# Where one copy stands in ScalarE's queue: the second expert layer of a decay-attention kernel

## The chip, the cores and the metric

The kernel runs on one core of a Trainium2 chip. A core has five engines with a queue of instructions each: TensorE (PE; its weight loads are listed as PEld), VectorE (DVE), ScalarE (ACT), GpSimd (POOL) and SyncE (SP), which issues the DMAs. Each works through its queue in order, and semaphores hold an instruction back until what it needs is there. The metric is the device time of one execution in microseconds (us), the median of several.

## The reference

Three steps follow each other, in float32: a linear attention with a decaying state, and two expert layers with different activations.

```python
for t in range(S):                                   # S = 768; 4 batches, 8 heads of 48
    cur = np.einsum('bhd,bhe->bhde', u[None] * kt, vt)
    y[:, :, t] = np.einsum('bhd,bhde->bhe', rt, state + cur)
    state = w[None, :, :, None] * state + np.einsum('bhd,bhe->bhde', kt, vt)
# x: 3072 tokens x 384
h = x @ w_in;  r = np.maximum(h, 0.0);  x = (r * r) @ w_out          # layer 1, d_ff 2048
h = x @ w_in2; g = h - np.tanh(h);      out = g @ w_out2             # layer 2, d_ff 2048
```

The change lies in layer 2 alone.

## The kernel before

The 3072 tokens are cut into NB = 6 blocks of TB = 512, and the 2048 hidden features into NF = 16 groups of 128. A **unit** is one block and one group: 96 units in layer 1, then 96 in layer 2. All matrix products are made of float32 numbers split into a rounded high part and the rest, the low part; a product then takes three terms: high by high, and the two mixed ones.

For a unit of layer 2, `gemm1` (L496) makes the hidden values h in a bank of PSUM, with nine matmuls of 128x512 (three slices of the 384 inputs, three terms). Three banks (3, 4, 5) take turns. `act2` turns h into g = h - tanh(h) and splits it; `gemm2_2` (L645) multiplies g by the second weights, nine matmuls again, and accumulates into three banks for the whole block. `evac2` (L656) copies these out at the end of a block, and SyncE writes them to memory.

Because h - tanh(h) loses its digits where h is small, `act2` computes two things and picks one. ScalarE makes y = h squared (L590), th = tanh(h) (L591), two shifted squares q1 (L593) and q2 (L596) and the sign of y - 0.25 as a mask (L599). VectorE makes hy = PK h y (L592), multiplies it by q1 + PC (L600) and by q2 + PD (L606), which is a polynomial in h for small values; it makes h - th (L595), and puts that over hy where the mask says so (L611). Then ScalarE rounds hy into the high part (L617, `act2_high`) and VectorE subtracts that to get the low part (L623, `act2_low`).

The work on one unit is spread over three calls of `act2`. In the call for unit n, L606 and L611 (`act2_poly`, `act2_pick`) and L617 work on unit n-1, and L623 on unit n-2. So ScalarE's queue in one call reads: y, th, q1, q2, mask of n, high part of n-1. VectorE's reads: L592 of n, L606 of n-1, L595 of n, L611 of n-1, L623 of n-2, L600 of n. `act2_flush` finishes the last unit.

The order on every queue is the order of the program text (`tc.manual_schedule()`). The waits are put in by the framework: an instruction waits for those before it in the text, on other engines, whose data it uses or whose buffer it takes over. `look` sets how far the first products run ahead in layer 2:

```python
while nf < len(units) and nf <= n + look(n):
    front(nf)          # gemm1 and act2 of unit nf; look is 3 in layer 2
    nf += 1
```

and after it, in the same round, comes `gemm2_2` of unit n. So TensorE's queue in a quiet stretch reads: first product of n+3, second of n, first of n+4, second of n+1.

Around that, `prep_x2` loads the next block's input in three slices and splits it, with a VectorE copy (L568) and a GpSimd subtraction (L569) in three of the 16 rounds (f = 5, 7, 9). In the first block's rounds f = 1 and 2 the last two weight tiles of layer 2 are still made (L101 on ScalarE, L107 on GpSimd). Buffers: hy has 3, y, th, q1, q2 and mask have 2 each, the high and low parts 4 each.

Of the kernel before, what the change touches and what calls it, by code (L numbers as in the profile page):

```python
# [13 lines left out]
ALU = mybir.AluOpType  # L14
# [5 lines left out]
PK = 0.0069430512315236536  # L20
# [5 lines left out]
def decay_attention_moe_moe_kernel(  # L26
# [10 lines left out]
    nc = tc.nc  # L37
# [464 lines left out]
    def split(g):  # L502
        hi = gp.tile([128, TB], F32R, tag="ghi", name="ghi", bufs=4)
        lo = gp.tile([128, TB], F32R, tag="glo", name="glo", bufs=4)
        return hi, lo
# [75 lines left out]
    def act2(j, f):  # L581
        pool = p2["pool"]
        h = hq.pop((2, j, f))
        n = j * NF + f
        mk = lambda n: pool.tile([128, TB], F32, tag=n, name=n)
        y, th, q1, q2 = (mk(n) for n in ("y", "th", "q1", "q2"))
        hy = pool.tile([128, TB], F32, tag="hy", name="hy", bufs=3)
        mask = pool.tile([128, TB], U8, tag="mask", name="mask")
        st2[n] = (q2, hy, mask, th)
        nc.scalar.activation(out=y, in_=h, func=AF.Square)  # L590
        nc.scalar.activation(out=th, in_=h, func=AF.Tanh)  # L591
        nc.vector.scalar_tensor_tensor(out=hy, in0=h, scalar=PK, in1=y, op0=ALU.mult, op1=ALU.mult)  # L592
        nc.scalar.activation(out=q1, in_=y, func=AF.Square, bias=p2["ba"], scale=1.0)  # L593
        act2_poly(n - 1)
        nc.vector.tensor_tensor(th, h, th, op=ALU.subtract)  # L595
        nc.scalar.activation(out=q2, in_=y, func=AF.Square, bias=p2["bb"], scale=1.0)  # L596
        act2_pick(n - 1)
        act2_low(n - 2)
        nc.scalar.activation(out=mask, in_=y, func=AF.Sign, bias=p2["bm"], scale=1.0)  # L599
        nc.vector.scalar_tensor_tensor(out=hy, in0=q1, scalar=PC, in1=hy, op0=ALU.add, op1=ALU.mult)  # L600
        act2_high(n - 1)

    def act2_poly(n):
        if n >= 0:
            q2, hy, mask, th = st2[n]
            nc.vector.scalar_tensor_tensor(out=hy, in0=q2, scalar=PD, in1=hy, op0=ALU.add, op1=ALU.mult)  # L606

    def act2_pick(n):
        if n >= 0:
            q2, hy, mask, th = st2[n]  # L610
            nc.vector.copy_predicated(hy, mask, th)  # L611

    def act2_high(n):
        if n >= 0:
            hy = st2[n][1]
            hi, lo = split(hy)
            nc.scalar.activation(out=hi, in_=hy, func=AF.Copy)  # L617
            st2[n] = (hy, hi, lo)

    def act2_low(n):  # L620
        if n >= 0:
            hy, hi, lo = st2.pop(n)
            nc.vector.tensor_tensor(lo, hy, hi.bitcast(F32), op=ALU.subtract)  # L623
            gq[(2, *divmod(n, NF))] = (hi, lo)

    def act2_flush():
        n = NB * NF - 1
        act2_poly(n)
        act2_low(n - 1)
        act2_pick(n)  # L630
        act2_high(n)
        act2_low(n)
# [57 lines left out]
    def front(n):  # L690
        layer, j, f = units[n]
        gemm1(layer, j, f)
        (act1 if layer == 1 else act2)(j, f)
        if n == len(units) - 1:
            act2_flush()
# [256 lines left out]
```

## Time and profile before

| | us |
|---|---|
| median of 3 runs | 962.3 (962.3 to 963.05) |
| the profiled execution, its own time | 963.27 |
| its span, first to last instruction | 961.5 |
| TensorE busy (matmul) | 922.7 |
| VectorE busy | 722.9 |
| ScalarE busy | 637.6 |
| GpSimd busy | 250.8 |
| mean granted TensorE clock | 0.988 |

The first row is what a change is measured by. The span leaves out 1.8 us around the first and last instruction of that execution. Busy times are sums over the whole span, in which the attention, layer 1 and layer 2 follow each other; layer 2 begins at about 527 us with its first product. An engine that is busy for most of the span need not be the one that sets the pace in each stage.

### The profile page before, as it was taken

Reading aid. Unit: us, or ns where it says so; the run is one execution under the profiler, and the core shown is the slowest. Engines: PE = TensorE matmul, PEld = TensorE weight load, DVE = VectorE, ACT = ScalarE, POOL = GpSimd, SP = SyncE. Lnnn points to the kernel's source line nnn. Section 1 sums busy time; section 2 is a strip of 40 time slices with the busy share of each in tenths; the row PEclk is TensorE's granted clock in tenths of the full one; section 3 lists DMA queues with packets and bytes.
Section 4 is the critical chain, followed back from the end, with each engine's and each line's share of the span. In section 5 each row is a group of like instructions: output and inputs, shape, how many; then the busy total and the mean of one; then the engine's idle time right before and its main releaser. Section 6 shows DMA issues by size and latency. Waiting matters only on the chain.

```text
span 961.5 us, 13137 instructions
## 1 busy us (share of the span) xinstructions
PE 922.7 (96%) x4748; PEld 741.5 (77%) x4748; DVE 722.9 (75%) x1201; ACT 637.6 (66%) x1150; POOL 250.8 (26%) x216
## 2 busy tenths in 40 slices
PE   7889999999999999999999999999999999999997
PEld 6767778888888888888888777777777777777775
DVE  6898957854882884550377789899899898898886
ACT  3656565555554554553688887877877887878885
POOL 5833325654563654443110011001000010010000
PEclk7999999999999999999999999999999999999999
DMA  8754512212121221201563100100100100100000
GB/s 248 232 168 159 191 59 65 87 52 77 54 93 38 85 60 49 79 7 40 199 230 132 55 12 1 56 11 1 56 12 1 55 12 1 56 11 1 34 1 33
DMA packets 28800, 67.50 MB, mean 70 GB/s; under 512 B 4928, under 2 KB 11968, under 8 KB 28736
## 3 DMA queue, kind: packets, MB, share of 16 engines
q1 hardware_dynamic: 28592, 66.47, 21.5%
q8 instruction: 37, 0.61, 0.3%
q10 hardware_dynamic: 144, 0.20, 0.1%
q14 instruction: 27, 0.22, 0.1%
HBM read 55.25 MB, written 9.44 MB: 67 GB/s over the span
## 4 chain that ended last, share of the span: by engine, by line
PE 45%; DVE 33%; ACT 17%; issue 2%; POOL 1%; DMA 1%; DVEq 0%; ACTq 0%; POOLq 0%
PE h L496 19%; PE acc L536 19%; DVE hy L592 7%; DVE hy L606 7%; DVE hy L611 7%; ACT ghi L617 6%; DVE th L595 6%; ACT th L591 5%; ACT y L590 5%; PE sc L290 2%; PE y L429 2%; PE y L422 2%; DVE w L107 1%; DVE am L342 1%; DVE raw L92 1%
## 5 line engine op out<-in xcount | busy, mean ns | idle before, releaser
L496 PE MATMUL h<-xt,w 128*128 128x512 f32 x864 | 215.9, 395 | 0.0
L496 PE MATMUL h<-xs,w 128*128 128x512 f32 x864 | 212.9, 391 | 0.0
L496 PEld LDWEIGHTS h<-xs,w 128*128 128x128 f32 x864 | 162.2, 188 | 36.2
L496 PEld LDWEIGHTS h<-xt,w 128*128 128x128 f32 x864 | 161.3, 190 | 33.8 <-DVE xt L406 0.4
L536 PE MATMUL acc<-ghi,w 128*128 128x512 f32 x576 | 153.3, 398 | 0.4 <-ACT x2s L552 0.4
L510 ACT ACTIVATE g<-h 128x512 f32<-128x512 f32 x96 | 57.2, 596 | 143.8 <-PE h L496 143.7
L645 PE MATMUL o<-ghi,w 128*128 128x512 f32 x576 | 150.6, 392 | 2.0 <-ACT ob L656 2.0
L645 PEld LDWEIGHTS o<-ghi,w 128*128 128x128 f32 x576 | 108.4, 189 | 26.5 <-ACT ob L656 4.1
L536 PEld LDWEIGHTS acc<-ghi,w 128*128 128x128 f32 x576 | 104.9, 188 | 23.9 <-ACT g L510 1.1
L516 POOL TENSOR_TENSOR glo<-g,ghi 128x512 fp32r<-128x512 f32 x64 | 85.7, 1339 | 136.2 <-ACT ghi L513 61.8
L617 ACT ACTIVATE ghi<-hy 128x512 fp32r<-128x512 f32 x96 | 60.7, 632 | 83.9 <-DVE hy L611 83.9
L569 POOL TENSOR_TENSOR xs<-x2f,xs 128x512 fp32r<-128x512 f32 x18 | 24.5, 1360 | 337.1 <-PE o L645 204.8
L592 DVE SCALAR_TENSOR_TENSOR hy<-h,y 128x512 f32<-128x512 f32 x96 | 66.4, 692 | 53.6 <-ACT th L591 53.5
L645 PE MATMUL o<-glo,w 128*128 128x512 f32 x288 | 93.1, 425 | 13.6 <-DVE glo L623 13.6
L536 PE MATMUL acc<-glo,w 128*128 128x512 f32 x288 | 84.5, 395 | 7.7 <-DVE glo L525 7.7
L645 PEld LDWEIGHTS o<-glo,w 128*128 128x128 f32 x288 | 47.9, 189 | 44.9 <-DVE glo L623 39.7
L324 POOL TENSOR_TENSOR am<-ident,bt 128x512 f32<-128x512 f32 x44 | 50.5, 1148 | 89.8 <-DVE bt L308 70.1
L606 DVE SCALAR_TENSOR_TENSOR hy<-q,hy 128x512 f32<-128x512 f32 x96 | 73.2, 763 | 0.1
L273 DVE TENSOR_TENSOR fr<-rkt,fr 112x256 fp32r<-112x256 f32 x30 | 38.8, 1294 | 42.9 <-ACT fr L272 42.9
L536 PEld LDWEIGHTS acc<-glo,w 128*128 128x128 f32 x288 | 54.0, 189 | 21.6 <-DVE glo L525 10.7
L611 DVE COPY_PREDICATED hy<-mask,th 128x512 f32<-128x512 uint8 x96 | 69.9, 728 | 0.0
L593 ACT ACTIVATE q<-y,ba 128x512 f32<-128x512 f32 x96 | 69.6, 725 | 0.0
(105 smaller groups left out, 1388.8 us busy)
## 6 DMA issues: line engine op xcount, KB each, us to landing
raw<-in_w_dram SPq DMA_DIRECT2D x32, 768.0 KB, 4.3
rkt<-in_rk_dram SPq DMA_DIRECT2D x23, 448.0 KB, 4.9
kvt<-in_nat_dram SPq DMA_DIRECT2D x23, 384.0 KB, 5.0
x2d<-x2s SPq DMA_DIRECT2D x18, 256.0 KB, 2.3
x2f<-x2d SPq DMA_DIRECT2D x18, 256.0 KB, 3.1
out_dram<-ob SPq DMA_DIRECT2D x18, 256.0 KB, 2.2
rnt<-in_nat_dram SPq DMA_DIRECT2D x23, 192.0 KB, 2.4
xt<-ys SPq DMA_DIRECT2D x120, 16.0 KB, 1.8
```

The source lines that it names most:

```text
L324: nc.gpsimd.tensor_tensor(am_t[d].rearrange("p (a z) t -> p a z t", a=2), ident[:, None, None, :].to_broadcast([128, 2, 2, C]), hd.to_broa ...
L496: nc.tensor.matmul(h, lhsT=w_in(layer, f, part, kk), rhs=x[:, xpart, kk, :], start=(n == 0), stop=(n == 3 * KK - 1),)
L510: nc.scalar.activation(out=g, in_=h, func=AF.Relu)
L516: nc.gpsimd.tensor_tensor(lo, g, hi.bitcast(F32), op=ALU.subtract)
L536: nc.tensor.matmul(acc[j][m], lhsT=w_out(1, f, part, m * 128, (m + 1) * 128), rhs=g, start=(f == 0 and n == 0), stop=(f == NF - 1 and n == 2),
L592: nc.vector.scalar_tensor_tensor(out=hy, in0=h, scalar=PK, in1=y, op0=ALU.mult, op1=ALU.mult)
L593: nc.scalar.activation(out=q1, in_=y, func=AF.Square, bias=p2["ba"], scale=1.0)
L595: nc.vector.tensor_tensor(th, h, th, op=ALU.subtract)
L606: nc.vector.scalar_tensor_tensor(out=hy, in0=q2, scalar=PD, in1=hy, op0=ALU.add, op1=ALU.mult)
L611: nc.vector.copy_predicated(hy, mask, th)
L617: nc.scalar.activation(out=hi, in_=hy, func=AF.Copy)
L645: nc.tensor.matmul(acc[j][m], lhsT=w_out(2, f, part, m * 128, (m + 1) * 128), rhs=g, start=(f == 0 and n == 0), stop=(f == NF - 1 and n == 2),
```

## The change

In `act2`, the call of `act2_high` moves from the end to the place behind the first Square, and works on unit n-2 in place of n-1. The VectorE instruction L592 is issued before the tanh in the text, where it was issued after it. `act2_flush` gets the call of `act2_high` that the last unit now lacks. ScalarE's queue in one call then reads: y of n, high part of n-2, th, q1, q2, mask of n. VectorE's queue keeps its order. The arithmetic is the same.

```diff
@@ -588,8 +588,9 @@
         mask = pool.tile([128, TB], U8, tag="mask", name="mask")
         st2[n] = (q2, hy, mask, th)
         nc.scalar.activation(out=y, in_=h, func=AF.Square)
+        act2_high(n - 2)
+        nc.vector.scalar_tensor_tensor(out=hy, in0=h, scalar=PK, in1=y, op0=ALU.mult, op1=ALU.mult)
         nc.scalar.activation(out=th, in_=h, func=AF.Tanh)
-        nc.vector.scalar_tensor_tensor(out=hy, in0=h, scalar=PK, in1=y, op0=ALU.mult, op1=ALU.mult)
         nc.scalar.activation(out=q1, in_=y, func=AF.Square, bias=p2["ba"], scale=1.0)
         act2_poly(n - 1)
         nc.vector.tensor_tensor(th, h, th, op=ALU.subtract)
@@ -598,7 +599,6 @@
         act2_low(n - 2)
         nc.scalar.activation(out=mask, in_=y, func=AF.Sign, bias=p2["bm"], scale=1.0)
         nc.vector.scalar_tensor_tensor(out=hy, in0=q1, scalar=PC, in1=hy, op0=ALU.add, op1=ALU.mult)
-        act2_high(n - 1)
 
     def act2_poly(n):
         if n >= 0:
@@ -625,6 +625,7 @@
 
     def act2_flush():
         n = NB * NF - 1
+        act2_high(n - 1)
         act2_poly(n)
         act2_low(n - 1)
         act2_pick(n)
```

## The prediction

> **What bounds the kernel now.** I read the page first, then busy time by stage, then the chain of waits in order of time, then the timeline of single units of layer 2.
>
> ```profile
> span 961.5 us, 13137 instructions
> ...
> PE 922.7 (96%) x4748; PEld 741.5 (77%) x4748; DVE 722.9 (75%) x1201; ACT 637.6 (66%) x1150; POOL 250.8 (26%) x216
> ...
> PE h L496 19%; PE acc L536 19%; DVE hy L592 7%; DVE hy L606 7%; DVE hy L611 7%; ACT ghi L617 6%; DVE th L595 6%; ACT th L591 5%; ACT y L590 5%; PE sc L290 2%; PE y L429 2%; PE y L422 2%; DVE w L107 1%; DVE am L342 1%; DVE raw L92 1%
> ...
> L592 DVE SCALAR_TENSOR_TENSOR hy<-h,y 128x512 f32<-128x512 f32 x96 | 66.4, 692 | 53.6 <-ACT th L591 53.5
> ```
>
> A TensorE (PE) that is busy 96% looks like the bound, but the chain holds no layer-2 matmul worth naming (L645 is absent): it runs through L590, L591, L592, L606, L595, L611 and L617, on ScalarE (ACT) and VectorE (DVE). By stages (columns: window, its length, then busy time of PE, PEld, DVE, ACT, POOL, granted clock, DMA share, GB/s):
>
> ```profile
> 461.00:531.00 70.00, 70.00 (x310) 57.96 (x309) 45.73 (x63) 56.28 (x85) 6.27 (x4) 1.00 0.47 167
> ...
> 684.20:754.50 70.30, 68.23 (x290) 52.82 (x288) 61.88 (x101) 56.44 (x100) 3.90 (x3) 1.00 0.07 23
> ...
> 895.00:957.50 62.50, 60.28 (x251) 46.96 (x250) 51.72 (x85) 47.48 (x84) 0.00 (x0) 0.97 0.04 13
> ```
>
> The end of layer 1 has no PE gap at a full clock; a block of layer 2 fits fewer matmuls (288 against some 310) into the same time. The chain in order of time gives both paces:
>
> ```profile
> 502.67 2.04 PE h L496 x9
> ...
> 684.24 1.56 ACT ob L656 x3
> 754.51 1.55 ACT ob L656 x3
> ```
>
> Nine matmuls in 2.04 us, 0.227 each, so a unit (18 matmuls) needs 4.08 us and a block of 16 units 65.3. A layer-2 block takes 754.51 - 684.24 = 70.27. Inside one unit (start, duration, engine, line, what; in brackets the idle time before it):
>
> ```profile
> 702.55 0.58 ACT L590 ACTIVATE y<-h 128x512 f32<-128x512 f32 x1
> ...
> 703.02 0.59 ACT L591 ACTIVATE th<-h 128x512 f32<-128x512 f32 x1
> ...
> 703.50 0.72 ACT L593 ACTIVATE q<-y,ba 128x512 f32<-128x512 f32 x1
> 703.64 0.69 DVE L592 SCALAR_TENSOR_TENSOR hy<-h,y 128x512 f32<-128x512 f32 x1 [0.50 <-ACT th L591]
> 704.12 0.72 ACT L596 ACTIVATE q<-y,bb 128x512 f32<-128x512 f32 x1
> 704.25 0.68 DVE L606 SCALAR_TENSOR_TENSOR hy<-q,hy 128x512 f32<-128x512 f32 x1
> 704.73 0.71 ACT L599 ACTIVATE mask<-y,bm 128x512 uint8<-128x512 f32 x1
> 704.85 0.68 DVE L595 TENSOR_TENSOR th<-h,th 128x512 f32<-128x512 f32 x1
> ...
> 705.45 0.73 DVE L611 COPY_PREDICATED hy<-mask,th 128x512 f32<-128x512 uint8 x1
> 706.08 0.68 DVE L623 TENSOR_TENSOR glo<-hy,ghi 128x512 fp32r<-128x512 f32 x1
> 706.22 0.63 ACT L617 ACTIVATE ghi<-hy 128x512 fp32r<-128x512 f32 x1 [0.77 <-DVE hy L611]
> 706.67 0.68 DVE L600 SCALAR_TENSOR_TENSOR hy<-q,hy 128x512 f32<-128x512 f32 x1
> 706.76 0.58 ACT L590 ACTIVATE y<-h 128x512 f32<-128x512 f32 x1
> 706.81 0.53 PEld L645 LDWEIGHTS o<-glo,w 128*128 128x128 f32 x3 [0.26 <-DVE glo L623]
> ```
>
> The period is 706.76 - 702.55 = 4.21, and it is a ring: L590, L591, then L592 (0.03 after tanh ends, not after the square ends at 703.13), L606, L595, L611, then L617 (0.04 after L611 ends), then the next L590. ScalarE stands idle 0.77 in it, VectorE 0.50, and PE waits at the low part because the ring is 0.13 slower than PE's 4.08.
>
> **The change part by part.** No instruction is added or removed. Three things move.
>
> *L617 one unit later.* It now follows L590 of unit n and works on unit n-2, whose L611 was issued a unit earlier, so the 0.77 wait is gone, and L590 no longer stands behind L611. Its consumers: L623 of n-2, four places later on VectorE in the same unit, and TensorE's product of n-2, which comes after two more groups of nine matmuls (4.08). The high part is ready 0.47 + 0.63 = 1.10 after L590 starts, so this hides; from 2.98 us of lateness of ScalarE on, each further one would be a stop of TensorE. The copy moved past no DMA: ScalarE and VectorE issue none here.
>
> *L592 ahead of tanh.* Its order on VectorE is as before; what changes is which of two readers of bank h goes first. I take it that L592 follows L590 at the measured 0.03, and that tanh, which reads the same bank, then waits for L592 to end at the measured 0.04. Queued behind tanh are q1, q2 and mask, and L595 waits for tanh on VectorE. From L592's start t:
>
> - ScalarE: tanh t + 0.69 + 0.04 = 0.73; then start to start 0.48, 0.62 and 0.61 to q1, q2, mask, and 0.61 to the next L590: 2.32 together. L590 to L592 is 0.61. Its ring: 0.73 + 2.32 + 0.61 = 3.66.
> - VectorE: L595 at 0.73 + 0.59 + 0.03 = 1.35 (without a wait 1.21), then 0.60 to L611, 0.63 to L623, 0.59 to L600, 0.60 to the next L592: 3.77.
>
> The trace of before doesn't show that reversed wait. Bounds: no wait at all makes VectorE 3.63; L592 waiting for L617 too is the first rival. I take 3.77, since the two readers stand one behind the other in all 96 units. The Trainium skill, "PSUM — Partial Sum Buffer", section "PSUM bank collisions raise a hardware error", says that ScalarE and VectorE may not touch one bank in the same partitions at once, reads against reads included. It speaks against the change, for the wait is then only turned round; by it the ring is 3.77, without it 3.63. The 0.03 agrees.
>
> Both are under 4.08, so **TensorE sets the pace**, with 0.31 per unit to recover from disturbances. The low part of n comes from unit n+2's stretch of VectorE work. After the first product of n+2, TensorE has nine matmuls (second product of n-1), nine (first of n+3) and six with the high part of n before it needs the low part: 24 x 0.227 = 5.44. It is ready 0.03 + 0.61 + (1.35 + 0.60 + 0.63) + 0.68 = 3.90 after it. So a unit may be 1.5 us late before TensorE stops.
>
> *Disturbances.* Evacuation of a block, the casts for the next block, and the last weight conversions:
>
> ```profile
> 613.97 1.55 ACT L656 ACTIVATE ob<-o 128x512 f32<-128x512 f32 x3
> ...
> 615.40 0.61 ACT L590 ACTIVATE y<-h 128x512 f32<-128x512 f32 x1
> ```
>
> ```profile
> 711.48 0.42 DVE L568 CAST xs<-x2f 128x512 fp32r<-128x512 f32 x1
> ...
> 712.06 0.69 DVE L592 SCALAR_TENSOR_TENSOR hy<-h,y 128x512 f32<-128x512 f32 x1 [0.16 <-ACT th L591]
> ...
> 712.67 1.22 DVE L606 SCALAR_TENSOR_TENSOR hy<-q,hy 128x512 f32<-128x512 f32 x1
> ```
>
> Evacuation costs ScalarE 1.43, so lateness 1.43 + 3.66 - 4.08 = 1.0, gone after four units: hidden. A cast costs VectorE 0.58, and L606 beside it 0.54 more: 1.12, three times at a distance of two units that recover 0.62. Lateness at the low part grows 0.8, 1.3, 1.8 and passes 1.5 by about 0.2: 0.2 x 4 blocks = 0.8. In the first block the conversions come on top:
>
> ```profile
> 551.62 0.89 ACT L101 ACTIVATE w<-raw 128x768 fp32r<-128x768 f32 x1
> ```
>
> Twice 0.89 on ScalarE before the earlier lateness is recovered: 0.9 with that block's casts.
>
> *Start and end of the layer.*
>
> ```profile
> 533.61 0.69 DVE L525 TENSOR_TENSOR glo<-g,ghi 128x512 fp32r<-128x512 f32 x1
> ...
> 536.09 4.26 PE L496 MATMUL h<-xs,w 128*128 128x512 f32 x18
> ...
> 540.19 1.52 PE L645 MATMUL o<-ghi,w 128*128 128x512 f32 x6
> ...
> 543.25 0.98 PE L645 MATMUL o<-glo,w 128*128 128x512 f32 x3 [1.53 <-DVE glo L623]
> ```
>
> Unit 1's L592 stands behind L525: 534.22. Tanh 534.95, evacuation 2.32 later, 537.27, three at 0.52, L590 of unit 2 at 538.8, low part of unit 0 at 538.8 + 0.61 + 2.58 + 0.68 = 542.7, wanted at 540.19 + 6 x 0.227 = 541.55: a stop of 1.2 (before 1.53).
>
> ```profile
> 943.66 2.21 PE L496 MATMUL h<-xs,w 128*128 128x512 f32 x9
> ...
> 951.12 0.69 DVE L600 SCALAR_TENSOR_TENSOR hy<-q,hy 128x512 f32<-128x512 f32 x1
> 951.26 0.96 PE L645 MATMUL o<-glo,w 128*128 128x512 f32 x3 [1.83 <-DVE glo L623]
> ...
> 951.91 0.69 DVE L606 SCALAR_TENSOR_TENSOR hy<-q,hy 128x512 f32<-128x512 f32 x1
> ...
> 957.53 0.39 PE L645 MATMUL o<-glo,w 128*128 128x512 f32 x1
> ```
>
> After the last first product (G) four second products remain, 8.16, and the chain shows: low of unit 93 at G + 3.9 (wanted 3.4), L600 at 3.8, L606 0.79 later, L623 5.2, L611 5.8, L617 6.6, L623 7.25 to 7.95; TensorE stops 0.5, 0.6 and 0.5 at these: 1.6.
>
> **The sum.** From 540.19 TensorE has the first products of 92 units (four are done: 96 less the rows before it) and 96 second ones: 188 x 2.04 = 383.5, ending with the last drain of 0.16 at 923.9. Stops: 1.2 + 0.9 + 0.8 + 1.6 = 4.5, end 928.4. Before it ended at 957.53 + 0.39 = 957.9. Gain 29.5, by which the profiled execution (963.27, span 961.5) becomes 933.8, span 932.0; the runs' median, 1 us lower, goes from 962.3 to **932.8**. Stops of 1.5 (no more than before's first) give 930; stops of 8, if each disturbance is counted twice, 936: its own range is 930 to 937.
>
> **Rivals.**
>
> *The wait is put on more than the square: L592 starts after L617* (the change doesn't do what it says). Then L592 comes 0.47 + 0.63 + 0.03 = 1.13 after L590, tanh at 1.86, and ScalarE's ring is 1.86 + 2.32 = 4.18, above TensorE's. A block: 16 x 4.18 + 1.43 + 3 x 0.16 = 68.8 against 70.27, over 417.7 / 70.27 = 5.9 blocks 8.7 gained: 953.6. For it: one L592 did wait for a later ScalarE instruction than its operand. Against: that one reads bank h, L617 doesn't.
>
> *VectorE's ring is slower than its sum* and lies between 4.08 and 4.21, because each handover costs more than 0.04. Nothing is recovered then: to the units of a block come the evacuation, 1.43, and the stretched L606, 3 x 0.54. At 4.15: 66.4 + 3.05 = 69.45 against 70.27, gain 0.82 x 5.9 = 5, time 957; at 4.10, 68.6 and 952. Against: hops of 0.03 to 0.04 in the unit above. The period of 3.77 holds two of them, which would have to cost 0.2 each.
>
> *Slower: the clock.* Layer 2 would hold TensorE, VectorE and ScalarE all near full, which no stage above does. The price is 383.5 / c: at a mean granted clock of 0.90 it is 426.1 + 4.5 against 417.7, time 975; it decides from 383.5 / (417.7 - 4.5) = 0.93 down. For it: 0.97 in the last stretch. Against: 1.00 with PE never idle from 461 to 531, and that 0.97 comes with PE's 1.8 us stop. The Trainium skill, "TensorE: Matmul & The Clock Gate", section "Part 1: The HAM clock gate", has the gate close on idleness and open on activity; by that rule fewer gaps can only raise the clock, as the two rows have it.
>
> **How the numbers follow.** Forecast 0.78; L592 behind L617 0.09; VectorE's ring 0.07; no effect to be seen 0.03; slower by the clock 0.03. Range 929 to 946: the forecast's own range, and part of the way to the second and third case, which leaves out about 0.2. A difference under 0.2% (1.9 us) can't be told from none here. Faster 0.94, same 0.03, slower 0.03.
>
> **What would show it.** Right: L617 without idle time before it, L591 waiting for L592 about 0.1 to 0.2 in each unit, L595 for L591 about 0.14; blocks of 65.3 to 65.8 between evacuations; L645 on the chain with the nine-row groups of layer 1; PE idle under 6 us after 540. Wrong: L592 starting at L617's end, a period over 4.1 in a quiet unit, DVE idle at L592 as large as before, or a granted clock under 0.98 in the middle of layer 2.

## The result and the profile after

The changed kernel takes 934.5 us (median of 4 runs, 934.33 to 935.4) against 962.67 for the kernel before: a ratio of 0.971, 95% interval 0.969 to 0.973. The forecast was 932.8, in a range of 929 to 946. The profiled execution took 935.4, with a span of 933.7, 27.8 less than before.

From the page of the changed kernel: span, busy time, and the chain of work that ended last, by engine and by line.

```profile
span 933.7 us, 13137 instructions
...
PE 907.2 (97%) x4748; PEld 745.8 (80%) x4748; DVE 729.7 (78%) x1201; ACT 642.6 (69%) x1150; POOL 251.2 (27%) x216
...
PE 86%; DVE 7%; ACT 3%; DMA 1%; issue 1%; POOL 1%; SPq 0%; DVEq 0%; ACTq 0%; POOLq 0%
PE h L496 39%; PE acc L536 20%; PE o L646 20%; PE sc L290 2%; PE y L429 2%; PE y L422 2%; DMA kvt<-in_nat_dram 1%; DVE am L342 1%; DVE rkt L254 1%; PE sc L300 1%; DVE rkt L253 1%; DVE glo L525 1%; PE y L438 1%; DVE hy L592 1%; DVE raw L93 0
```

From the list of groups by line (busy time and mean ns of one, then the idle time before them and what ended it), the copy and the two instructions that changed places:

```profile
L592 DVE SCALAR_TENSOR_TENSOR hy<-h,y 128x512 f32<-128x512 f32 x96 | 66.0, 687 | 13.5 <-ACT y L590 13.4
...
L617 ACT ACTIVATE ghi<-hy 128x512 fp32r<-128x512 f32 x96 | 60.1, 626 | 2.3 <-DVE hy L611 2.3
L593 ACT ACTIVATE th<-h 128x512 f32<-128x512 f32 x96 | 57.5, 599 | 41.9 <-DVE hy L592 41.9
```

(Line numbers from tanh on have moved: tanh is L593, q1 L594, h - th L596, q2 L597, mask L600, the multiplication by q1 L601, the second product L646, the evacuation L657. L617 and L623 are as before.) The chain has become TensorE's: both products of layer 2 are in it now (L496, which serves both layers, has 39%, L646 20%), and of layer 2's lines on VectorE and ScalarE only L592 is still listed, with 1%. The idle time before the copy is 2.3, all of it at the last unit, where the page of before had 83.9:

```profile
L617 ACT ACTIVATE ghi<-hy 128x512 fp32r<-128x512 f32 x96 | 60.7, 632 | 83.9 <-DVE hy L611 83.9
```

Instead, tanh has a wait of 41.9 that it did not have. By stages (columns as in the prediction):

```profile
674.40:739.90 65.50, 65.50 (x289) 53.85 (x288) 62.79 (x100) 57.17 (x100) 3.88 (x3) 1.00 0.08 25
...
871.00:930.00 59.00, 58.12 (x253) 46.69 (x251) 52.93 (x84) 48.75 (x84) 0.00 (x0) 1.00 0.04 14
```

A block of layer 2 takes 65.5 and has no PE gap that these windows show; before it took 70.3. One unit in its timeline:

```profile
694.93 0.60 ACT L590 ACTIVATE y<-h 128x512 f32<-128x512 f32 x1 [0.29 <-PE h L496]
695.42 0.62 ACT L617 ACTIVATE ghi<-hy 128x512 fp32r<-128x512 f32 x1
695.56 0.69 DVE L592 SCALAR_TENSOR_TENSOR hy<-h,y 128x512 f32<-128x512 f32 x1 [0.21 <-ACT y L590]
...
696.29 0.60 ACT L593 ACTIVATE th<-h 128x512 f32<-128x512 f32 x1 [0.24 <-DVE hy L592]
...
696.92 0.69 DVE L596 TENSOR_TENSOR th<-h,th 128x512 f32<-128x512 f32 x1
...
699.01 0.60 ACT L590 ACTIVATE y<-h 128x512 f32<-128x512 f32 x1 [0.29 <-PE h L496]
```

The period is 699.01 - 694.93 = 4.08, TensorE's. ScalarE now waits for TensorE (0.29 before the square). L592 starts 0.03 after the square ends, while the copy still runs; tanh starts 0.04 after L592 ends. L592 to L596 is 1.36 (forecast 1.35).

### The profile page after: what moved, and what is told of

Its sections match the earlier page's. It is cut to its first block, busy times and chain, and to the rows that moved or that the text cites. A ratio compares the mean times of both kernels' runs of the same rounds, so it can differ in the third digit from the quotient of the medians.

```text
span 933.7 us, 13137 instructions
## 1 busy us (share of the span) xinstructions
PE 907.2 (97%) x4748; PEld 745.8 (80%) x4748; DVE 729.7 (78%) x1201; ACT 642.6 (69%) x1150; POOL 251.2 (27%) x216
## 4 chain that ended last, share of the span: by engine, by line
PE 86%; DVE 7%; ACT 3%; DMA 1%; issue 1%; POOL 1%; SPq 0%; DVEq 0%; ACTq 0%; POOLq 0%
PE h L496 39%; PE acc L536 20%; PE o L646 20%; PE sc L290 2%; PE y L429 2%; PE y L422 2%; DMA kvt<-in_nat_dram 1%; DVE am L342 1%; DVE rkt L254 1%; PE sc L300 1%; DVE rkt L253 1%; DVE glo L525 1%; PE y L438 1%; DVE hy L592 1%; DVE raw L93 0%
## 5 line engine op out<-in xcount | busy, mean ns | idle before, releaser
L496 PE MATMUL h<-xt,w 128*128 128x512 f32 x864 | 215.6, 394 | 0.0
L496 PE MATMUL h<-xs,w 128*128 128x512 f32 x864 | 211.4, 389 | 0.0
L496 PEld LDWEIGHTS h<-xs,w 128*128 128x128 f32 x864 | 162.2, 188 | 34.0
L496 PEld LDWEIGHTS h<-xt,w 128*128 128x128 f32 x864 | 161.0, 190 | 33.5
L646 PE MATMUL o<-ghi,w 128*128 128x512 f32 x576 | 148.8, 390 | 0.3 <-ACT ghi L617 0.3
L646 PEld LDWEIGHTS o<-ghi,w 128*128 128x128 f32 x576 | 107.7, 188 | 24.0 <-ACT ob L657 1.3
L593 ACT ACTIVATE th<-h 128x512 f32<-128x512 f32 x96 | 57.5, 599 | 41.9 <-DVE hy L592 41.9
L646 PE MATMUL o<-glo,w 128*128 128x512 f32 x288 | 84.2, 394 | 2.0 <-DVE glo L623 1.9
L606 DVE SCALAR_TENSOR_TENSOR hy<-q,hy 128x512 f32<-128x512 f32 x96 | 78.2, 814 | 0.1
L592 DVE SCALAR_TENSOR_TENSOR hy<-h,y 128x512 f32<-128x512 f32 x96 | 66.0, 687 | 13.5 <-ACT y L590 13.4
L596 DVE TENSOR_TENSOR th<-h,th 128x512 f32<-128x512 f32 x96 | 66.2, 689 | 5.9 <-ACT th L593 0.7
L611 DVE COPY_PREDICATED hy<-mask,th 128x512 f32<-128x512 uint8 x96 | 70.8, 737 | 0.0
L594 ACT ACTIVATE q<-y,ba 128x512 f32<-128x512 f32 x96 | 68.7, 715 | 0.0
```

The source lines that it names most:

```text
L496: nc.tensor.matmul(h, lhsT=w_in(layer, f, part, kk), rhs=x[:, xpart, kk, :], start=(n == 0), stop=(n == 3 * KK - 1),)
L646: nc.tensor.matmul(acc[j][m], lhsT=w_out(2, f, part, m * 128, (m + 1) * 128), rhs=g, start=(f == 0 and n == 0), stop=(f == NF - 1 and n == 2),
```

## The experiments

Each run changes one thing against the kernel before or the changed one; ratios are to the kernel before, with 95% intervals.

### Which of the two moves brought the gain

The copy alone (tanh ahead of L592 again):

```diff
         nc.scalar.activation(out=y, in_=h, func=AF.Square)
         act2_high(n - 2)
-        nc.vector.scalar_tensor_tensor(out=hy, in0=h, scalar=PK, in1=y, op0=ALU.mult, op1=ALU.mult)
         nc.scalar.activation(out=th, in_=h, func=AF.Tanh)
+        nc.vector.scalar_tensor_tensor(out=hy, in0=h, scalar=PK, in1=y, op0=ALU.mult, op1=ALU.mult)
```

> Only the copy L617 moves (high part one unit later); VectorE's first operation stays behind tanh. Theory (the ring through L617 was the bound, TensorE is now): ScalarE has no wait left, 3.33 us per unit, VectorE 3.63, so the quiet unit is TensorE's 4.08 and nearly the whole gain is here. But L592 starts 1.6 us after L590 in place of 0.6, so the low part is ready about 4.8 us after TensorE asks for it, of 5.44: only 0.7 us of lateness is covered, and casts and evacuations stop TensorE more often. Time 935 to 941, most likely 937.5, some 3 us above both moves together. Rival (the gain comes from VectorE's head start of half a microsecond before tanh): the period stays near 4.2, time 955 to 962.

And L592 alone, in the kernel before:

```diff
-        nc.scalar.activation(out=th, in_=h, func=AF.Tanh)
         nc.vector.scalar_tensor_tensor(out=hy, in0=h, scalar=PK, in1=y, op0=ALU.mult, op1=ALU.mult)
+        nc.scalar.activation(out=th, in_=h, func=AF.Tanh)
```

> Only VectorE's first operation goes ahead of tanh; L617 stays at the end of ScalarE's call, for unit n-1. Theory: tanh waits for L592 (0.73 after it starts), then 0.48 + 0.62 + 0.61 + 0.61 to the copy, 0.54 to the next square, 0.61 to the next L592: ScalarE's ring is 4.20, as long as before's 4.21, and only the casts are hidden better. Quiet unit 4.18 to 4.22, time 955 to 962, most likely 957. Rival (the head start is what counts): quiet unit 4.08 and a time of 935 to 940.

Measured: the copy alone 943.3 us, 0.980 (0.978 to 0.982); L592 alone 957.2, 0.994 (0.993 to 0.996). Of 28 us, the copy by itself brings 19.5, L592 by itself 5.6, and 3 come only with both. L592 alone is where it was expected. Its timeline:

```profile
692.45 0.69 DVE L591 SCALAR_TENSOR_TENSOR hy<-h,y 128x512 f32<-128x512 f32 x1 [0.32 <-ACT y L590]
...
693.18 0.60 ACT L592 ACTIVATE th<-h 128x512 f32<-128x512 f32 x1 [0.76 <-DVE hy L591]
...
695.51 0.62 ACT L617 ACTIVATE ghi<-hy 128x512 fp32r<-128x512 f32 x1
...
696.65 0.69 DVE L591 SCALAR_TENSOR_TENSOR hy<-h,y 128x512 f32<-128x512 f32 x1 [0.31 <-ACT y L590]
```

The period is 696.65 - 692.45 = 4.20, as worked out: the wait of 0.77 before the copy is now a wait of 0.76 before tanh. Moving one operation only carried the idle time along ScalarE's queue; the copy in that place is what fills it.

The copy alone was 2.3 us above its expected range, though its quiet unit is 4.08 like the changed kernel's (ScalarE's squares start at 694.44 and 698.52). Rows of its first block, around a weight conversion and around the end of the block:

```profile
554.90 1.86 POOL L107 TENSOR_TENSOR w<-raw,w 128x768 fp32r<-128x768 f32 x1 [1.93 <-ACT w L101]
555.25 2.10 DVE L611 COPY_PREDICATED hy<-mask,th 128x512 f32<-128x512 uint8 x1
557.97 0.96 PE L646 MATMUL o<-glo,w 128*128 128x512 f32 x3 [2.01 <-DVE glo L623]
...
606.51 0.61 PE L646 MATMUL o<-ghi,w 128*128 128x512 f32 x2
607.42 0.50 PE L646 MATMUL o<-glo,w 128*128 128x512 f32 x1 [0.30 <-DVE glo L623]
```

With tanh ahead, L592 starts a microsecond later after the square, the low part comes later, and less lateness is covered. ("Cover" is how late a low part may be before TensorE has to wait for it.) At the conversion TensorE stops for 2.0 (0.34 in the changed kernel). There the longer hold-up by GpSimd comes on top: under its subtraction for the weights (L107), L611 takes 2.10 in place of 0.73, and one unit earlier L601 took 2.38 in place of 0.68; in the changed kernel the same subtractions meet L606, with 1.38 and 1.62 in place of 0.68. How much of the 2.0 is the later L592 and how much the longer hold-up, no run here separates. The stop at the end of the block was overlooked in the expectation. The last second product of a block is sorted by output bank, so it asks for the low part after two matmuls and not after six. That takes 4 x 0.227 = 0.9 from the cover, more than the 0.7 that the copy alone leaves, and stops TensorE in every block. So what the copy alone lacks against both moves, 9 us, would be mostly cover and not pace; the next runs test that.

### Whether the head start of L592 is cover: the first product four units ahead

```diff
     def look(n):
-        return 1 if n < NF - 2 else 2 if n < NB * NF else 3
+        return 1 if n < NF - 2 else 2 if n < NB * NF else 4
```

With both moves, and with the copy alone:

> Both moves, and TensorE's first product runs four units ahead in layer 2 instead of three. Theory (what is left above TensorE's own 4.08 per unit is stops at the low part after disturbances and at both ends of the layer, 5.7 us by the profile of the changed kernel): nine more matmuls lie between, lateness of 3.6 us is covered instead of 1.5, so blocks of 65.3 and stops of 1 us or less at the start and the end: 929 to 931. Rival (TensorE's blocks are longer than 65.3 for another reason, or the third PSUM bank for h is then taken too early): 934 or slower.

> Only the copy L617 moves, with the first product four units ahead. Theory (L592 ahead of tanh brings only an earlier low part, which is slack and not pace): the same time as both moves with four units ahead, 928.5 to 931. Rival (L592 ahead of tanh is worth something in the pace): still some 3 us slower than that, 933 or more.

Measured: 935.5 us, 0.972 (0.970 to 0.973), with both; 934.6, 0.971 (0.969 to 0.973), with the copy alone. The two are alike, so the 9 us between the copy alone and both moves are gone once TensorE runs further ahead: the head start of L592 is cover. But neither is faster than the changed kernel; both expectations (929 to 931 and 928.5 to 931) were missed. With both moves the stops at the low part did vanish; one stop came in their place, at the first evacuation:

```profile
608.19 0.61 PE L646 MATMUL o<-ghi,w 128*128 128x512 f32 x2
612.37 1.19 PE L646 MATMUL o<-ghi,w 128*128 128x512 f32 x4 [3.57 <-ACT ob L657]
...
614.63 3.26 PE L496 MATMUL h<-xs,w 128*128 128x512 f32 x9
```

The third matmul of the next block needs the bank that ScalarE evacuates first, and ScalarE was so late that TensorE stood 3.6 us. After it nine matmuls took 3.26 in place of 2.20: the granted clock fell as well (0.63 from 612.3 to 616.9). With three units ahead, TensorE's small stops at the low part had let ScalarE make up its lateness in the first block; with four, the lateness was kept and paid at once. The traces bear this out: from the fifth to the sixteenth unit of that block, a unit's square starts 3.5 to 4.8 us after the recorded end of its first product in this run, and 0.2 to 1.4 us in the changed kernel.

So: four units ahead only from the second block on, with both moves, and with the copy alone.

```diff
-        return 1 if n < NF - 2 else 2 if n < NB * NF else 4
+        return 1 if n < NF - 2 else 2 if n < NB * NF else 3 if n < NB * NF + NF else 4
```

> Both moves; TensorE's first product runs three units ahead in the first block of layer 2 and four from the second block on. Theory (with four units ahead from the start, lateness that TensorE's stops used to let ScalarE make up was kept until the first evacuation, which then held up TensorE for 3.7 us and cost it clock besides; from the second block on VectorE keeps pace): no such stop, blocks of 65.3, an end with 0.5 us of stops in place of 1.5: 931 to 933. Rival (evacuations stop TensorE in each block when ScalarE works one unit further behind): stops of over 1 us before the third matmul of a block's first second product, 934 or more.

> Only the copy L617 moves; four units ahead from the second block on. Theory (the head start of L592 is slack and not pace): the first block costs some 3 us more than with both moves, as it did with three units ahead, and all later blocks take 65.3: 934 to 936. Rival (the head start belongs to the pace): blocks near 66.7 as with the copy moved alone, 940 or more.

> The changed kernel itself, for the comparison on one chip: 934 to 935.5 by every theory.

On one chip: 933.9 (0.971, 0.969 to 0.972) with both, 936.7 (0.973, 0.972 to 0.975) with the copy alone, 935.6 (0.972, 0.971 to 0.974) for the changed kernel. The intervals overlap. Both came out some 1 us above their expectations. The run with both moves kept one large stop after the first block, at the second evacuation. The run with the copy alone lost clock after its stop of 2.0 in the first block, stopped once more for 0.30 at the end of that block, and from the second block on ran without a stop until the end of the layer. First a row of the one, then two answers of the other (timeline, then a later block by stage):

```profile
678.88 1.21 PE L646 MATMUL o<-ghi,w 128*128 128x512 f32 x4 [0.95 <-ACT ob L657]
```

```profile
557.61 0.96 PE L646 MATMUL o<-glo,w 128*128 128x512 f32 x3 [2.01 <-DVE glo L623]
558.41 3.81 PE L496 MATMUL h<-xs,w 128*128 128x512 f32 x9
```

```profile
675.00:740.00 65.00, 65.00 (x288) 53.83 (x287) 62.05 (x100) 56.65 (x100) 3.90 (x3) 1.00 0.08 25
```

This suggests a mixture: L592 ahead of tanh in the first block, where cover is short, and behind it later, where four units ahead cover enough and VectorE's shorter ring makes up lateness faster.

```diff
-        nc.vector.scalar_tensor_tensor(out=hy, in0=h, scalar=PK, in1=y, op0=ALU.mult, op1=ALU.mult)
+        if j == 0:
+            nc.vector.scalar_tensor_tensor(out=hy, in0=h, scalar=PK, in1=y, op0=ALU.mult, op1=ALU.mult)
         nc.scalar.activation(out=th, in_=h, func=AF.Tanh)
+        if j:
+            nc.vector.scalar_tensor_tensor(out=hy, in0=h, scalar=PK, in1=y, op0=ALU.mult, op1=ALU.mult)
```

> The copy L617 moved everywhere; L592 ahead of tanh in the first block of layer 2 alone; four units ahead from the second block on. Theory (the head start of L592 is cover against lateness, needed while three units ahead is all there is; with four units ahead VectorE's shorter ring of 3.63 is worth more): the first block as in the changed kernel, 68.4, then blocks of 65.3 without a stop at evacuations, 0.5 us of stops at the end: 2 us less than the changed kernel, 931.5 to 933.5. Rival (the head start belongs to the pace): blocks over 66, 936 or more.

> The changed kernel itself beside it on the same chip: 934 to 936 by every theory.

Measured on one chip: 933.8 (932.8 to 934.4 in 5 runs), 0.970 (0.969 to 0.972), against 935.1 (934.8 to 935.8 in 4 runs), 0.972 (0.971 to 0.973). The mixture is 0.3 above its expected range. From the first second product to the last matmul of layer 2 the mixture takes 928.50 - 540.60 = 387.9 and the changed kernel 930.02 - 540.44 = 389.6:

```profile
540.60 1.52 PE L649 MATMUL o<-ghi,w 128*128 128x512 f32 x6
...
928.10 0.40 PE L649 MATMUL o<-glo,w 128*128 128x512 f32 x1
```

```profile
540.44 1.52 PE L646 MATMUL o<-ghi,w 128*128 128x512 f32 x6
...
929.63 0.39 PE L646 MATMUL o<-glo,w 128*128 128x512 f32 x1
```

The profile has 1.7 of the 2 us expected, the medians 1.2. Of the kernels here that compute the whole output it has the lowest median. Its five times lie below the four beside it, but the difference is below 0.2% and the intervals of the ratios overlap: not settled by timing.

### What bounds before and after

Three of nine matmuls are left out of each first product of layer 2 (the low part of the weights times the high part of x, so the output lacks that term), first in the changed kernel, then in the kernel before:

```diff
-        terms = [(part, kk, xpart) for part in range(2) for kk in range(KK) for xpart in range(2 - part)]
+        terms = [(part, kk, xpart) for part in range(2 if layer == 1 else 1) for kk in range(KK) for xpart in range(2 - part)]
...
-                start=(n == 0), stop=(n == 3 * KK - 1),
+                start=(n == 0), stop=(n == len(terms) - 1),
```

> The changed kernel with three of nine matmuls left out of each first product of layer 2 (the low part of the weights times the high part of x; the output lacks this term). TensorE then needs 3.40 us per unit. Theory (VectorE's ring of 3.77 is next, and casts at 0.58 + 0.79 and evacuations no longer find room): quiet unit 3.77, a block 16 x 3.77 + 1.3 + 3 x 1.37 = 65.7 at most and hardly shorter than now, time 925 to 932, most likely 928. Rival (TensorE alone sets the time and the ring has room to spare): 96 x 0.68 = 65 less, about 870.

> The kernel before, with the same three matmuls left out of each first product of layer 2. Theory (before was bound by the ring of ScalarE and VectorE at 4.21): quiet unit 4.21, blocks of 70.2, time 959 to 962.5. Rival (TensorE's 96% busy was the bound): 96 x 0.68 = 65 less, about 897.

Measured: 928.9 us, 0.965 (0.962 to 0.967), for the changed kernel, and 961.5, 0.9993 (0.998 to 1.0005), for the kernel before. Leaving out a third of the first products, 65 us of TensorE's work, brought the kernel before nothing: its unit stayed at 706.38 - 702.17 = 4.21, by ScalarE's timeline.

```profile
702.17 0.58 ACT L590 ACTIVATE y<-h 128x512 f32<-128x512 f32 x1
706.38 0.58 ACT L590 ACTIVATE y<-h 128x512 f32<-128x512 f32 x1
```

The changed kernel gained 6 us and no more. Two of its units, and two of its evacuations in the chain of waits:

```profile
690.32 0.69 DVE L592 SCALAR_TENSOR_TENSOR hy<-h,y 128x512 f32<-128x512 f32 x1
...
694.11 0.70 DVE L592 SCALAR_TENSOR_TENSOR hy<-h,y 128x512 f32<-128x512 f32 x1
```

```profile
673.20 1.46 ACT ob L657 x3
737.87 1.46 ACT ob L657 x3
```

VectorE's ring is 694.11 - 690.32 = 3.79 (worked out: 3.77), and a block 64.67 with its disturbances. So after the change TensorE needs 65.3 per block and VectorE, with the wait for tanh in its ring, 64.7: the next bound lies 1% below the new one.

Then the tanh in that kernel reads y in place of h, so that it does not touch PSUM (the output is that of another function besides):

```diff
-        nc.scalar.activation(out=th, in_=h, func=AF.Tanh)
+        nc.scalar.activation(out=th, in_=y, func=AF.Tanh)
```

> As the run with three matmuls fewer per unit, and tanh reads y instead of h (it computes the tanh of h squared, so the output is another function). Tanh then reads no PSUM. Theory (tanh waits for L592 only because both read one bank): the wait of ScalarE before tanh is gone, VectorE's ring falls from 3.77 to 3.63, blocks get 2 to 3 us shorter and the time is 907 to 917. Rival (tanh waits for VectorE for another reason, or VectorE's ring does not hang on tanh): the same wait, the same time as with three matmuls fewer alone.

Measured: 908.9 us, 0.944 (0.941 to 0.947). Tanh's wait is gone, by the list of groups, and a block fell to 726.03 - 664.52 = 61.5, by 3.2 (expected 2 to 3):

```profile
L593 ACT ACTIVATE th<-y 128x512 f32<-128x512 f32 x96 | 59.6, 621 | 0.1
```

```profile
664.52 1.45 ACT ob L657 x3
726.03 1.45 ACT ob L657 x3
```

Tanh waits for L592 because both read h, and for nothing else. (h is one tile in one bank of PSUM; whether the tile or the bank counts, this run does not tell apart.) That is the rule of the Trainium skill, "PSUM — Partial Sum Buffer", section "PSUM bank collisions raise a hardware error", by which two engines' reads of one bank have to be kept apart; this run agrees, with a wait of 49.3 us in the kernel beside it and 0.1 here.

## Why the prediction was right

*What bounds the kernel.* Shown: TensorE, 96% busy, was not the bound of layer 2 before (the same time with a third of its first products gone), and it is now (blocks of 65.5, TensorE busy throughout), with VectorE close behind.

*L617 one unit later.* Right, and it is the larger part: 19.5 us alone.

*L592 ahead of tanh.* The reversed wait was priced right (1.36 from L592 to L596 against 1.35, a ring of 3.79 against 3.77, and 4.20 with this move alone). What the prediction did not say, and the runs show, is its part in the gain: it does not set the pace with the copy moved, since then 4.08 is reached without it; it brings cover, worth some 9 us at three units ahead (at the first block's conversions mixed with the hold-up by GpSimd) and nothing to be seen at four.

*Disturbances and ends.* The sum had 388.2 us from the first second product to the last matmul; the trace has 930.06 - 540.49 = 389.6. Rows of the changed kernel's TensorE timeline:

```profile
534.68 0.50 PE L536 MATMUL acc<-glo,w 128*128 128x512 f32 x1 [0.93 <-DVE glo L525]
...
540.49 1.52 PE L646 MATMUL o<-ghi,w 128*128 128x512 f32 x6
...
542.99 0.96 PE L646 MATMUL o<-glo,w 128*128 128x512 f32 x3 [0.98 <-DVE glo L623]
...
560.27 0.98 PE L646 MATMUL o<-glo,w 128*128 128x512 f32 x3 [0.34 <-DVE glo L623]
...
924.12 0.96 PE L646 MATMUL o<-glo,w 128*128 128x512 f32 x3 [0.59 <-DVE glo L623]
...
929.66 0.40 PE L646 MATMUL o<-glo,w 128*128 128x512 f32 x1
```

Measured start to start against 0.227 per matmul, so with what a restart loses: the start 1.26 (term 1.2); the first block 1.6 (0.9), of which 0.9 lies after the two conversions, at 555.56 and 560.27, and 0.6 at two casts; a later block 0.26 (0.2), so 1.1 for four (0.8); the end 1.8 (1.6). Together 5.8 against 4.5: the term for the first block was the one sized too small. It priced a conversion by ScalarE's 0.89 alone. But GpSimd's part of the conversion (L107) holds up VectorE too, and more so in the changed kernel, where L606 starts sooner under it. First the changed kernel, then the kernel before:

```profile
555.73 2.12 POOL L107 TENSOR_TENSOR w<-raw,w 128x768 fp32r<-128x768 f32 x1 [2.59 <-ACT w L101]
...
556.77 1.62 DVE L606 SCALAR_TENSOR_TENSOR hy<-q,hy 128x512 f32<-128x512 f32 x1
```

```profile
559.33 0.89 DVE L606 SCALAR_TENSOR_TENSOR hy<-q,hy 128x512 f32<-128x512 f32 x1
```

At the two conversions L606 takes 1.38 and 1.62 in place of 0.68, so 1.6 us in all, against 0.90 and 0.89 before. In the second, L596, L611 and L623 follow it without a gap, and TensorE's stop ends with that L623. What the first block would have cost without this, no run shows. About 0.1 of a later block's 0.26 lies at the evacuation, which the prediction had as hidden: the third matmul of a block's first second product comes about 0.1 late there, its weight load waiting for L657.

Another 0.3 went ahead of the sum's start: unit 0's tanh now waits for L592, its L596 ends later, and L525, behind it on VectorE, holds up layer 1's last second product for 0.93 where it was 0.63. The run with L592 alone has the 0.93 too, the one with the copy alone 0.63.

*The casts* were priced right by luck, by two errors that cancel:

```profile
699.35 0.43 DVE L568 CAST xs<-x2f 128x512 fp32r<-128x512 f32 x1
...
699.68 0.69 DVE L592 SCALAR_TENSOR_TENSOR hy<-h,y 128x512 f32<-128x512 f32 x1
699.91 1.29 POOL L569 TENSOR_TENSOR xs<-x2f,xs 128x512 fp32r<-128x512 f32 x1 [47.30 <-DVE xs L568]
...
700.28 1.47 DVE L606 SCALAR_TENSOR_TENSOR hy<-q,hy 128x512 f32<-128x512 f32 x1
```

A cast takes 0.33 of VectorE's time, not 0.58: the row of before held a wait for tanh. L606 is stretched by 0.79, not 0.54, because with that wait gone it starts earlier under GpSimd's subtraction. Both make 1.12.

*The rivals.* L592 waiting for L617: refuted by its start, 0.03 after the square and while the copy runs. VectorE's ring above its sum: refuted, 3.79 where it is the bound. The clock: 1.00 in the windows of layer 2, in the last stretch too, where before had 0.97. In no trace did the clock of layer 2 fall without a stop of TensorE just before it.

## What to carry to other kernels

A ring is a circle of waits through two engines that sets the period though neither engine is busy all the time. It is broken where one of them waits for an operation that could as well be done on an older unit; moving another operation past the wait only carries the idle time along, as the run with L592 alone shows (0.76 in place of 0.77). Taking work out of the new bound shows how far the next one lies: here 1% below. And work ahead of the bound is paid for where it must come together again, here at the evacuation: running further ahead hid every small stop and made one large one.

## What was not expected of the hardware

A VectorE operation with both inputs in SBUF is held up while GpSimd's subtraction runs, by nearly the time that is left of it: 0.79 where 0.92 was left (701.20 - 700.28), and before the change 0.54 where 713.33 - 712.67 = 0.66 was left, with GpSimd's row of before at

```profile
712.03 1.30 POOL L569 TENSOR_TENSOR xs<-x2f,xs 128x512 fp32r<-128x512 f32 x1 [51.19 <-PE o L645]
```

L592, one of whose two inputs lies in PSUM, keeps its 0.69 under it: before the change it starts at 712.06, after the subtraction's 712.03. The Trainium skill, "SBUF — State Buffer", section "Who interferes with whom", has it so: a VectorE instruction with two SBUF inputs contends with a GpSimd instruction that reads SBUF; one with a single SBUF input, outside VectorE's modes that use both ports, does not.

Stops of TensorE of about 2 us went both ways. After 2.01 (the copy alone, four units ahead from the second block), 2.05 (the copy alone, four ahead throughout), 1.83 (the end of the kernel before) and 1.86 (the same place with three matmuls fewer), about eight matmuls started 0.43 apart in place of 0.227, at a cost of some 1.6 us; the granted clock was 0.56 from 558.4 to 562.3 in the first of these. After 2.01 with the copy alone and 1.85 with L592 alone TensorE kept its pace (in the former, the nine matmuls that followed took 2.21). The stop of 3.6 cost 1.6 as well. No stop of 1.6 or less in layer 2 was followed by a lower clock. What decides between the two cases at 2 us, no run here shows.
